# The hand-over from the dense layer to the experts: one weight load issued by ScalarE, one conversion and two squarings queued behind the last tile's routing

## The chip, the cores and the metric

The kernel runs on one core of a Trainium2 chip. The metric is device time in microseconds (us) of one execution, and the time of a version is the median of several executions. Besides, one execution was recorded by the hardware profiler; its trace gives the start and duration of the instructions on each engine: TensorE (PE, with its weight loads shown apart as PEld), VectorE (DVE), ScalarE (ACT), GpSimd (POOL) and SyncE (SP, which issues DMAs here). Three engines issue DMAs: SP (the queue called q1 in the trace), ACT (q10) and POOL (q0).

## The reference, cut to what matters

The computation is a chain of three layers on 1152 tokens: an attention with a top-32 mask, a dense gated layer, and a routed layer with 8 experts, of which each token goes to one. Only the routed layer and what stands just ahead of it bear on the change:

```
logits = x @ w_gate                       # x: 1152 x 512, 8 experts
expert_idx = argmax(logits, axis=1)
gate_w = probs[arange(N), expert_idx]     # probs = softmax(logits)
# each token gets the next free place of its expert: disp[e, counts[e]] = x[i]
h = maximum(einsum('ecd,edf->ecf', disp, w1), 0.0)     # w1: 8 x 512 x 1024
y = einsum('ecf,efd->ecd', h, w2)                      # w2: 8 x 1024 x 512
out[i] = gate_w[i] * y[expert_idx[i], pos[i]]
```

## The kernel before, in words

The tokens are worked in nine tiles of 128 rows (NT = 9). For each tile there is attention, then `norm`, then the dense layer `moe1`, then `dispatch`, which routes the tile's tokens. Instructions are given to a scheduler that fixes one order for each engine when the program is built; on the chip each engine then works strictly in that order and waits where data are missing. `tc.issue_after(ins)`, here wrapped as `after(t, name)`, puts what is traced inside it behind `ins` in the order of the engine of `ins`; it touches no other engine and waits for no result.

**Routing.** `dispatch(t)` transposes the layer's output (L490) and copies it (`xu`, L492, on ACT), multiplies it with the router (L504, PE), copies the logits (`lg`, L507, DVE), and finds the chosen expert: the maximum (L527), its place as a one-hot row (`key`, `k8`, `oh`, L534 to L541), the place in the expert's list by two small matmuls against the counts (`before`, `cum`, L544 and L545, PE), and the row number `slot` (L565). Beside it runs the softmax weight (`nm`, `ex` L532 on ACT, L550, L553, L556) and the row itself: its size by a square on ACT (L498), a power of two from it (L511 to L517), the upper half `yh` (L519, ACT) and the lower half `yl` (L520, DVE). When row and slot are there, GpSimd scatters the 128 rows to the table `disp` in DRAM (L567). The last tile (t = 8) does most of this on DVE, earlier tiles partly on GpSimd.

**First expert.** The rows of expert 0 that earlier tiles have put into its first 128 places (group "a") don't wait for the last tile: `gather("a", ...)` (L775, a transposing DMA, issued by ACT behind `xu`) and `notes("a", ...)` (L788, the rows' weights and token numbers, ACT as well) read them during the last tile's routing. Those that the last tile adds (group "b", at most 48 rows) are fetched after its scatter: POOL gathers them (`xb`, L830), SP transposes them (`xbT`, L834).

**Weights.** The 16 expert matrices (2 MB each, two per expert) are loaded in the order `ORDER`, called weights 0 to 15 here, each as two DMAs of 1 MB (`load`, L721, all issued by SP). `size(j, n)` squares a matrix on ACT (L734), sums over partitions on PE (L739) and makes a power of two on DVE (L737 to L749). `convert(j, n)` splits it into two float16 halves: the upper half partly on ACT (L759) and partly on DVE (L761), the lower half on DVE (L764). Weights 0 to 3 are converted in four pieces each (2 pieces at L759, 2 at L761, 4 at L764), later ones in two (1, 1 and 2). The raw buffer of weights n is free for weights n + 4 once it is converted; weights 4 take the buffer of weights 2, weights 5 that of weights 3. `fetch_w` issues the next load; SP's order after weights 4 is the gathers of experts 1 to 3 with `xbT` between them, and then weights 5 onward (`issue_after(last.ins)`).

**Products.** `up` and `down` are the two products of an expert (L847, PE), evacuated by ACT (`hE`, L857) and DVE (L858; `yT`, L866). PE's order at the hand-over is `up("a")`, `down("a")`, `up("b")`, `up(1)`, `down("b")`, `up(2)`, `down(1)` and so on, with `send` (transposes L885, ACT L887, a scatter to the output by POOL L889) between them.

Of the kernel before, what the change touches and what calls it, by code (L numbers as in the profile page):

```python
# [14 lines left out]
AF = mybir.ActivationFunctionType  # L15
OP = mybir.AluOpType
# [5 lines left out]
DM = H * D  # L22
# [3 lines left out]
NT = N // P  # L26
# [10 lines left out]
WA = 128  # L37
# [8 lines left out]
def tile_topk_attention__then__moe__then__moe_routed(  # L46
# [3 lines left out]
    nc = tc.nc  # L50
    w_gate, w_val, w_out = (a.bitcast(I32) for a in (w_gate, w_val, w_out))
    cap = int(capacity)
# [5 lines left out]
    disp = dram.tile([E * cap + 16, ROW], F32, name="disp")  # L58
# [364 lines left out]
    yx, late, behind = {}, [], {}  # L423

    def after(t, engine):

        return tc.issue_after(behind[t, engine].ins)
# [58 lines left out]
    def dispatch(t):  # L486
        y = yx.pop(t)
# [6 lines left out]
        yh, yl = (yd[:, i * DM // 2:(i + 1) * DM // 2].bitcast(F16) for i in range(2))  # L494
        nc.gpsimd.tensor_copy(yd[:, DM + 1:ROW], tok[:, t:t + 1])
        yn = route.tile([P, 8], F32, name="yn")
# [19 lines left out]
            invert(yn[:, 2:3], yn[:, 1:2])  # L516
        nc.vector.tensor_scalar(yn[:, 5:6], yn[:, 1:2], YS, None, op0=OP.mult)  # L517
        if t == NT - 1:
            nc.scalar.activation(yh, y, AF.Copy, scale=yn[:, 5:6])  # L519
            nc.vector.scalar_tensor_tensor(yl, y, yn[:, 5:6], yh, op0=OP.mult, op1=OP.subtract)  # L520
        else:
            nc.scalar.activation(y, y, AF.Copy, scale=yn[:, 5:6])
            nc.scalar.activation(yh, y, AF.Copy)
            nc.gpsimd.tensor_tensor(yl, y, yh, op=OP.subtract)
# [15 lines left out]
        ev = nc.vector if t == NT - 1 else nc.gpsimd  # L540
# [6 lines left out]
        pos = route.tile([P, 4], F32, name="pos")  # L547
# [10 lines left out]
        if t == NT - 1:  # L558
            nc.vector.tensor_scalar(had, lp[:, 2, 0:1], float(WA), None, op0=OP.min)
            nc.vector.tensor_scalar(rest, had, tok[:, 0:1], cap - 1.0, op0=OP.add, op1=OP.min)  # L560
            with after(t, "xu"):
                gather("a", 0, 0, WA, ew, nc.scalar)
                notes("a", 0, 0, WA, ew, nc.scalar)
        slot = route.tile([P, 1], I32, name="slot")
        ev.tensor_scalar(slot, pos[:, 0:1], pos[:, 1:2], pos[:, 2:3], op0=OP.add, op1=OP.add)  # L565
        nc.gpsimd.tensor_tensor(cum, cum, oh, op=OP.add)
        scat.append(nc.gpsimd.indirect_dma_start(  # L567
            out=disp, out_offset=bass.IndirectOffsetOnAxis(ap=slot[:, :1], axis=0),
# [73 lines left out]
    for p in range(NP):  # L642
        t, hp = divmod(p, 4)
# [12 lines left out]
    for t in range(NT):  # L656
        ew = nc.vector if t in (0, 8) else nc.gpsimd
        t0 = (4 * t + 5) * SL
        at(t0 + 1, ahead(norm(t, ew), 300), 1)
        at(t0 + (12 if t < NT - 1 else 18), ahead(moe1(t, ew), 0), 2.7)  # L660
        at(t0 + 10 + 4 * SL, ahead(dispatch(t), 0), 3 if t < NT - 1 else 1)
    live = []
    slot = 0
# [23 lines left out]
    ew = ctx.enter_context(tc.tile_pool(name="ew", bufs=1, reuse_waits="tile"))  # L687
# [7 lines left out]
    ORDER = [0, 1, 2, 3, 4]  # L695
# [13 lines left out]
    def raw_of(n):  # L709

        if n < 2:
            return slots[2 + n]
        return raws[n % 2 if n < 4 else n % 4]

    def load(j, n):
        e, w = divmod(j, 2)
        src = (w1, w2)[w][e].rearrange("(c p) f -> p c f", p=P)
        dst = raw_of(n).rearrange("p (c f) -> p c f", c=src.shape[1])
        m = src.shape[1] // 2
        for g in range(2):  # L720
            nc.sync.dma_start(dst[:, g * m:(g + 1) * m], src[:, g * m:(g + 1) * m])  # L721

    sized = {}
    BIG = 4 * DM
# [27 lines left out]
    def convert(j, n):  # L752

        raw, (hi, lo), sc = raw_of(n), place(j), sized.pop(j)
        k = 4 if n < 4 else 2
        for g in range(k):
            r = slice(g * 2 * BIG // k, (g + 1) * 2 * BIG // k)
            if 2 * g < k:
                nc.scalar.activation(hi[:, r], raw[:, r], AF.Copy, scale=sc[:, 7:8])  # L759
            else:  # L760
                nc.vector.tensor_scalar(hi[:, r], raw[:, r], sc[:, 7:8], None, op0=OP.mult)  # L761
        for g in range(k):
            r = slice(g * 2 * BIG // k, (g + 1) * 2 * BIG // k)
            nc.vector.scalar_tensor_tensor(lo[:, r], raw[:, r], sc[:, 7:8], hi[:, r], op0=OP.mult, op1=OP.subtract)  # L764

    meta, every, xgT, hE, yT2 = {}, {}, {}, {}, {}
# [3 lines left out]
    def gather(k, e, lo, hi, pool, eng):  # L770

        r = e * cap + lo
        n = -(-(hi - lo) // 16) * 16
        xgT[k] = pool.tile([P, 2 * KC, n], F16, name="xgT", bufs=1 if pool is ew else 3)
        g = eng.dma_start_transpose(out=xgT[k], in_=disp.bitcast(F16)[r:r + n, :2 * DM])  # L775
        return g

    def notes(k, e, lo, hi, pool, eng):

        for i, (o, m) in enumerate(chunks(hi - lo)):  # L780
            x = pool.tile([P, E, 2], F32, name=f"notes{i}", bufs=1 if pool is ew else 2)
            if k == 1 and not lo:
                eng.dma_start(x[:m, 1:], disp[:E * cap].rearrange("(e c) d -> c e d", c=cap)[lo + o:lo + o + m, 1:, DM:])
                every[i] = x
                for f in range(1, E):
                    meta[f, i] = x[:, f]
            else:
                eng.dma_start(x[:m, e], disp[e * cap + lo + o:e * cap + lo + o + m, DM:])  # L788
                meta[k, i] = x[:, e]

    def chunks(n):
        return [(o, min(P, n - o)) for o in range(0, n, P)]

    loaded = [0]

    def fetch_w():
        n = loaded[0]
        loaded[0] += 1
        if n < 2 * E:
            load(ORDER[n], n)  # L800

    for n in range(4):
        fetch_w()
# [10 lines left out]
    convert(1, 1)  # L814
    with after(NT - 1, "dve"):
        convert(2, 2)
    fetch_w()
    size(3, 3)
    pacc = ctx.enter_context(tc.tile_pool(name="pacc", bufs=3, space=PSUM, reuse_waits="tile"))
    pback = ctx.enter_context(tc.tile_pool(name="pback", bufs=2, space=PSUM, reuse_waits="tile"))  # L820
# [29 lines left out]
    def up(k, e, n):  # L850
        hE[k] = [eb.tile([P, NF2, n], F16, name=f"hE{i}", bufs=2 if n <= W else 1) for i in range(2)]
        for lo, hi in groups(NF2, n):
            a = pacc.tile([P, hi - lo, n], F32, name="acc")
            for c in range(lo, hi):
                product(a[:, c - lo, :], place(2 * e), (xgT[k][:, :KC], xgT[k][:, KC:]), KC, F2, c)
            hh, hl = (x[:, lo:hi, :] for x in hE[k])
            nc.scalar.activation(hh, a, AF.Relu)  # L857
            nc.vector.scalar_tensor_tensor(hl, a, 0.0, hh, op0=OP.max, op1=OP.subtract)  # L858
# [35 lines left out]

    with after(NT - 1, "pe"):
        up("a", 0, WA)
    with after(NT - 1, "dve"):
        convert(3, 3)
    last = gather(1, 1, 0, W, eb, nc.sync)
    rest_gather()  # L900
    notes(1, 1, 0, W, eb, nc.sync)
    for e in range(2, 4):
        last = gather(e, e, 0, W, eb, nc.sync)
# [5 lines left out]
    def ready():  # L909

        n = done[0]
        done[0] += 1
        if n >= 2 * E:
            return
        if n == 4:
            with after(NT - 1, "act"):
                size(ORDER[4], 4)
        if n + 1 < 2 * E:
            size(ORDER[n + 1], n + 1)
        convert(ORDER[n], n)  # L920
        fetch_w()
# [93 lines left out]
```

## Time and profile before

| | |
|---|---|
| median of 3 runs | 698.01 us (697.99 to 699.74) |
| the profiled execution | 697.47 us, of which its span is 695.6 us |
| busy in the span | PE 552.8, PEld 401.2, DVE 612.3, ACT 497.0, POOL 438.2 us |
| DMA | 80.00 MB, mean 115 GB/s over the span |
| granted TensorE clock, mean | 0.932 |

The span is what the trace covers; the profiled execution has 1.87 us more than its span. Times below count from the span's start. Busy time is an average over the three layers, so the rows are read stage by stage: the hand-over lies between about 540 and 575 us, the experts' products after it.

### The profile page before, as it was taken

The page shows a single profiled execution, that of the slowest core. Times are in us where ns is not written, and L with a number is a line of the kernel's source. Part 1 is how long each engine was busy: PE and PEld are TensorE (multiplying, and loading weights), DVE is VectorE, ACT ScalarE, POOL GpSimd, SP SyncE. Part 2 cuts the span into 40 slices and gives each one's busy share as a digit, 9 for nine tenths or more (in the row PEclk, how much of TensorE's full clock was granted, in tenths as well). Part 3 has the DMA queues.
Part 4 walks back from the last instruction along what each step waited for, and adds up shares of the span by engine and source line. Part 5 has one row for each costly group of instructions (what it writes and reads, how often), then busy time and mean ns, then how long its engine had stood idle before and what let it go on. Part 6 is the DMA issues. An engine that isn't in the chain of part 4 may idle for free.

```text
span 695.6 us, 12985 instructions
## 1 busy us (share of the span) xinstructions
PE 552.8 (79%) x4708; PEld 401.2 (58%) x4708; DVE 612.3 (88%) x1215; ACT 497.0 (71%) x959; POOL 438.2 (63%) x521
## 2 busy tenths in 40 slices
PE   1217425467687999999999999999999679999994
PEld 1106314344444666666666666665545469999994
DVE  3999999999999999999999999997158865999960
ACT  3456539569875888878789787887598438988821
POOL 3785889988895987877878779597531110023312
PEclk9999665588989999999999999999999889999998
DMA  8998171475000001000000000000850459999201
GB/s 236 264 327 279 34 243 44 128 228 192 17 1 23 9 31 43 16 32 10 31 8 16 32 9 24 1 2 16 302 197 1 151 125 389 309 328 347 96 21 39
DMA packets 47016, 80.00 MB, mean 115 GB/s; under 512 B 18732, under 2 KB 23340, under 8 KB 46946
## 3 DMA queue, kind: packets, MB, share of 16 engines
q1 hardware_dynamic: 43954, 74.02, 33.5%
q0 software_dynamic: 1792, 4.83, 1.9%
q8 instruction: 39, 0.64, 0.4%
q10 hardware_dynamic: 1200, 0.26, 0.2%
q14 instruction: 31, 0.25, 0.1%
HBM read 64.35 MB, written 12.27 MB: 110 GB/s over the span
## 4 chain that ended last, share of the span: by engine, by line
PE 31%; DVE 24%; issue 14%; POOL 13%; ACT 9%; DMA 7%; SPq 1%; POOLq 0%; ACTq 0%; DVEq 0%
PE pm L450 9%; PE pm L475 6%; DVE r L331 6%; DVE m L334 6%; PE acc L847 4%; POOL pp L351 3%; DVE wbig L155 3%; PE xps L382 3%; DMA wbig<-in_w_out_dram 3%; DVE wbig L157 3%; PE tp L374 2%; POOL out_dram L889 2%; PE tp L308 2%; DVE m L322 2%; DVE wbig L226 2%
## 5 line engine op out<-in xcount | busy, mean ns | idle before, releaser
L450 PE MATMUL pm<-wbig,xn 128*128 128x512 f16 x600 | 154.3, 390 | 6.9 <-ACT xn L420 3.5
L334 DVE MAX8 m<-r 128x8 f32<-128x576 f32 x216 | 156.5, 743 | 0.4
L847 PEld LDWEIGHTS <-split 128*128 128x128 f16 x1728 | 116.7, 100 | 13.7 <-issue 7.2
L308 PE MATMUL tp<-kst,qh 128*128 128x288 f32 (+1 forms) x160 | 64.2, 413 | 65.5 <-ACT s L310 21.4
L351 POOL TENSOR_TENSOR pp<-s,pp 128x576 f32<-128x576 f32 x72 | 102.9, 1442 | 10.1 <-ACT pp L350 9.6
L331 DVE MATCH_REPLACE8 r<-m,r 128x576 f32<-128x576 f32 x144 | 106.1, 738 | 0.0
L450 PEld LDWEIGHTS <-xn 128*128 128x128 f16 x648 | 63.4, 100 | 73.0 <-issue 14.2
L308 PEld LDWEIGHTS tp<-kst,qh 128*128 128x128 f32 (+1 forms) x160 | 32.6, 206 | 92.0 <-ACT s L310 29.0
L475 PE MATMUL pm<-wbig,hT 128*128 128x512 f16 x324 | 77.4, 380 | 7.3 <-DVE wbig L226 4.6
L310 ACT ACTIVATE s<-tp 128x288 f32<-128x288 f32 x144 | 54.7, 410 | 22.3 <-POOL pp L351 18.3
L889 POOL DMA_INDIRECT out_dram<-ob,tos x14 | 22.5, 1609 | 71.6 <-ACT ob L887 56.2
L764 DVE SCALAR_TENSOR_TENSOR split<-raw,sc,split 128x2048 f16<-128x2048 f32 (+1 forms) x32 | 65.8, 2077 | 0.3 <-ACT split L759 0.3
L374 PE MATMUL tp<-ident,pp 128*128 128x128 f32 x324 | 56.7, 294 | 11.0 <-ACT pp L356 10.5
L350 ACT ACTIVATE pp<-s,bias 128x576 f32<-128x576 f32 x72 | 51.9, 772 | 16.0 <-POOL bias L336 15.9
L847 PE MATMUL acc<-hE,split 128*128 128x168 f16 (+2 forms) x864 | 58.8, 228 | 4.0 <-ACT junk L734 1.3
L847 PE MATMUL acc<-xgT,split 128*128 128x168 f16 (+1 forms) x768 | 58.0, 239 | 4.3 <-DMA xgT<-disp 4.3
L734 ACT ACTIVATE junk<-raw 128x2048 bf16<-128x2048 f32 (+1 forms) x32 | 54.1, 1692 | 6.8 <-DMA raw<-in_w_dram 5.7
L356 ACT ACTIVATE pp<-pp,bias 128x576 f32<-128x576 f32 x72 | 56.3, 782 | 3.2 <-POOL pp L351 2.9
L375 ACT ACTIVATE pt<-tp 128x384 f32<-128x384 f32 x108 | 48.8, 492 | 11.7 <-PE tp L374 6.9
L374 PEld LDWEIGHTS tp<-ident,pp 128*128 128x128 f32 x324 | 41.3, 150 | 25.0 <-ACT pp L356 13.8
L382 PE MATMUL xps<-pt,vt 128*64 128x128 f32 (+1 forms) x800 | 55.7, 279 | 0.0
L322 DVE MAX8 m<-s 128x8 f32<-128x576 f32 x72 | 53.6, 745 | 1.8 <-ACT s L310 1.7
(203 smaller groups left out, 1230.4 us busy)
## 6 DMA issues: line engine op xcount, KB each, us to landing
raw<-in_w_dram SPq DMA_DIRECT2D x28, 1024.0 KB, 9.8
wbig<-in_w_out_dram SPq DMA_DIRECT2D x6, 1024.0 KB, 9.0
disp<-wraw SPq DMA_DIRECT2D x18, 257.0 KB, 5.4
qraw<-in_q_l_dram SPq DMA_DIRECT2D x72, 64.0 KB, 2.2
wraw<-in_w_gate_dram SPq DMA_DIRECT2D x8, 512.0 KB, 4.5
split<-in_w_dram SPq DMA_DIRECT2D x4, 1024.0 KB, 7.6
kraw<-in_k_l_dram SPq DMA_DIRECT2D x12, 288.0 KB, 4.1
wbig<-in_w_val_dram SPq DMA_DIRECT2D x3, 1024.0 KB, 8.0
```

The costliest lines, as they stand in the source:

```text
L308: nc.tensor.matmul(sp[:c1], x[:, i, :c1], kst[b, hp][:, i, c * HALF:(c + 1) * HALF], start=(n == 0), stop=(n == 1))
L322: nc.vector.max(m[:, i, 0], s[i])
L331: nc.vector.match_replace(r[i], m[:, i, n - 1], src, -3.0e38)
L334: nc.vector.max(m[:, i, n], r[i])
L351: nc.gpsimd.tensor_tensor(w, s[i], w, op=OP.subtract)
L356: nc.scalar.activation(pp[p][:, i], pp[p][:, i], AF.Exp, bias=bias[:, i, 0:1], scale=0.125, accum_out=sums[t][:, h:h + 1])
L374: nc.tensor.transpose(tp[:, i, :], p2[:, o:o + P], ident)
L382: nc.tensor.matmul(xps[t][rows, hp, c0:c1], v, w, start=(n == 0), stop=(n == 4))
L450: nc.tensor.matmul(a, xn[:, x + c, :], half(i, lo), start=(c == 0 and n == 0), stop=(c == KC - 1 and n == 2))
L475: nc.tensor.matmul(yps, hT[f // KC][:, KC * hi + f % KC, :], half(i, lo), start=(f == 0 and n == 0), stop=(f == NF1 - 1 and n == 2))
L764: nc.vector.scalar_tensor_tensor(lo[:, r], raw[:, r], sc[:, 7:8], hi[:, r], op0=OP.mult, op1=OP.subtract)
L847: nc.tensor.matmul(a, u[:, c, col * P:(col + 1) * P], v[:, c, :a.shape[-1]], start=(c == 0 and n == 0), stop=(c == nk - 1 and n == 2))
```

## The change

Four things are done. The load of weights 4 is issued by ACT instead of SP, and in ACT's order it is put behind the notes of group "a". The conversion of weights 3 was traced behind the last tile's last half `hT` (`behind[t, "dve"]`), and is now traced behind `slot`; as `slot` is an instruction of DVE, this moves DVE's pieces alone. The squares of weights 4 on ACT are put behind `yh` as well as behind `ex`. The rest of the diff hands out the instructions that these lines need.

```diff
@@ -516,7 +516,7 @@
         if t == NT - 1:
-            nc.scalar.activation(yh, y, AF.Copy, scale=yn[:, 5:6])
+            behind[t, "yh"] = nc.scalar.activation(yh, y, AF.Copy, scale=yn[:, 5:6])
             nc.vector.scalar_tensor_tensor(yl, y, yn[:, 5:6], yh, op0=OP.mult, op1=OP.subtract)
@@ -560,9 +560,9 @@
             with after(t, "xu"):
                 gather("a", 0, 0, WA, ew, nc.scalar)
-                notes("a", 0, 0, WA, ew, nc.scalar)
+                behind[t, "notes"] = notes("a", 0, 0, WA, ew, nc.scalar)
         slot = route.tile([P, 1], I32, name="slot")
-        ev.tensor_scalar(slot, pos[:, 0:1], pos[:, 1:2], pos[:, 2:3], op0=OP.add, op1=OP.add)
+        behind[t, "slot"] = ev.tensor_scalar(slot, pos[:, 0:1], pos[:, 1:2], pos[:, 2:3], op0=OP.add, op1=OP.add)
@@ -712,13 +712,13 @@
-    def load(j, n):
+    def load(j, n, eng=nc.sync):
...
         for g in range(2):
-            nc.sync.dma_start(dst[:, g * m:(g + 1) * m], src[:, g * m:(g + 1) * m])
+            eng.dma_start(dst[:, g * m:(g + 1) * m], src[:, g * m:(g + 1) * m])
@@ -781,23 +781,24 @@
-                every[i] = x
+                every[i], d = x, None
...
-                eng.dma_start(x[:m, e], disp[e * cap + lo + o:e * cap + lo + o + m, DM:])
+                d = eng.dma_start(x[:m, e], disp[e * cap + lo + o:e * cap + lo + o + m, DM:])
                 meta[k, i] = x[:, e]
+        return d
...
-    def fetch_w():
+    def fetch_w(eng=nc.sync):
         n = loaded[0]
         loaded[0] += 1
         if n < 2 * E:
-            load(ORDER[n], n)
+            load(ORDER[n], n, eng)
@@ -814,7 +815,8 @@
     with after(NT - 1, "dve"):
         convert(2, 2)
-    fetch_w()
+    with after(NT - 1, "notes"):
+        fetch_w(nc.scalar)
     size(3, 3)
@@ -894,7 +896,7 @@
     with after(NT - 1, "pe"):
         up("a", 0, WA)
-    with after(NT - 1, "dve"):
+    with after(NT - 1, "slot"):
         convert(3, 3)
@@ -913,7 +915,7 @@
         if n == 4:
-            with after(NT - 1, "act"):
+            with after(NT - 1, "act"), after(NT - 1, "yh"):
                 size(ORDER[4], 4)
```

## Rows read from the trace of the kernel before

**Rows 1.** The chain that ended last: start us, duration us, what

```profile
546.09 5.96 DMA xgT<-disp
...
560.12 1.06 POOL disp L567
...
563.27 4.42 DMA xb<-disp,rest
567.71 3.06 DMA xbT<-xb
```

**Rows 2.** Timeline of DVE: start us, us, line, operation, count

```profile
542.14 1.64 DVE L761 TENSOR_SCALAR split<-raw,sc 128x1024 f16<-128x1024 f32 x2
543.70 2.47 DVE L764 SCALAR_TENSOR_TENSOR split<-raw,sc,split 128x1024 f16<-128x1024 f32 x2
546.09 1.40 DVE L761 TENSOR_SCALAR split<-raw,sc 128x1024 f16<-128x1024 f32 x2
547.41 4.86 DVE L764 SCALAR_TENSOR_TENSOR split<-raw,sc,split 128x1024 f16<-128x1024 f32 x4
...
552.26 2.46 DVE L764 SCALAR_TENSOR_TENSOR split<-raw,sc,split 128x1024 f16<-128x1024 f32 x2
554.65 0.15 DVE L507 COPY lg<-px 128x8 f32<-128x8 f32 x1
554.73 0.13 DVE L874 CAST to<-notes 128x1 int32<-128x1 f32 x1
...
555.50 0.23 DVE L541 TENSOR_SCALAR oh<-rank,k 128x8 bf16<-128x8 f32 x1
...
558.42 0.26 DVE L565 TENSOR_SCALAR slot<-pos 128x1 int32<-128x1 f32 x1
558.60 0.74 DVE L520 SCALAR_TENSOR_TENSOR yd<-yx,yn,yd 128x512 f16<-128x512 f32 x1
```

**Rows 3.** Timeline of PE in the same stretch; in brackets idle before it

```profile
546.73 1.06 PE L504 MATMUL px<-rg,xu 128*128 128x8 f32 x8 [0.69 <-ACT xu L492]
...
557.80 0.17 PE L545 MATMUL px<-cum,ones 128*128 128x8 bf16 x1
...
561.96 4.79 PE L847 MATMUL acc<-hE,split 128*128 128x128 f16 x83 [0.55 <-DVE sc L742]
570.81 3.69 PE L847 MATMUL acc<-xbT,split 128*128 128x48 f16 x96 [4.05 <-DMA xbT<-xb]
```

**Rows 4.** Timeline of ACT in the same stretch

```profile
547.48 0.60 ACTq L788 DMA_DIRECT2D notes<-disp  x1
...
557.59 0.71 ACT L519 ACTIVATE yd<-yx,yn 128x512 f16<-128x512 f32 x1
```

**Rows 5.** Timeline of SP's DMA issues, asked in several stretches

```profile
546.23 0.37 SPq L721 DMA_DIRECT2D raw<-in_w_dram  x1
...
552.30 0.37 SPq L721 DMA_DIRECT2D raw<-in_w_dram  x1
...
570.51 12.36 SPq L721 DMA_DIRECT2D raw<-in_w_dram  x8
```

**Rows 6.** DMA issues by line from 500 us on: size, median us to landing

```profile
disp<-yd,slot POOLq DMA_INDIRECT x3, 2.9
...
notes<-disp ACTq DMA_DIRECT2D x1, 1.0 KB, 4.8
```

**Rows 7.** The same for the gather of expert 3 alone

```profile
xgT<-disp SPq DMA_TRANSPOSE x1, 3.8
```

**Rows 8.** Stretches: us, PE, PEld, DVE, ACT, POOL busy, PEclk, DMA share, GB/s

```profile
572.00:576.00 4.00, 4.00 (x92) 3.99 (x90) 0.56 (x1) 1.18 (x2) 0.00 (x0) 0.77 0.99 346
...
600.00:604.00 4.00, 4.00 (x60) 4.00 (x58) 3.90 (x11) 3.33 (x5) 0.00 (x0) 1.00 1.01 400
```

**Rows 9.** PE: the later product of group "b", and a later gap

```profile
582.65 1.72 PE L847 MATMUL acc<-hE,split 128*128 128x48 f16 x62
...
608.08 2.19 PE L847 MATMUL acc<-hE,split 128*128 128x168 f16 x28 [1.34 <-ACT junk L734]
```

## The prediction, made before the changed kernel was run

> **What bounds the kernel now.** I read the chain of waits first, then the timelines of DVE, PE, ACT and SP around the hand-over from the dense layer to the experts, then the landing times and the stretches after it. The chain shows one hand-over with little work in it: a gather of 5.96 us that PE waits for, then the last tile's scatter, its 4.42 us gather and its 3.06 us transposing DMA [rows 1]. PE's timeline gives the price: before the first product of group "b" it stands still for 4.05 us, until that DMA lands at 570.77 [rows 1, 3]. The stretches say how things stand later: from 572 us on PE, DVE and DMA are all close to full (at 600 to 604 us PE 4.00 and DVE 3.90 of 4 us, DMA share 1.01), so a start that comes earlier is worth something only if all three begin earlier [rows 8].
>
> Why is the scatter as late as 560.12? PE has the logits at 546.73 + 1.06 = 547.79 [rows 3]. DVE copies them at 554.65, because it first works off pieces of weights 2 and 3 without a pause: 4 at L761 and 8 at L764 [rows 2]. SP's second half of weights 4 goes out at 552.30, just as a piece ends on DVE; that load needs weights 2's buffer, so a piece of weights 2 came as late as 552.2, and pieces of weights 3 lie before it: the two are interleaved, and half of the twelve pieces are weights 3 [rows 2, 5].
>
> **The change part by part.**
>
> *Conversion of weights 3 behind `slot`.* Half of the 12 pieces leave the stretch. Start to start, L761 takes (547.41 - 546.09) / 2 = 0.66 us and L764 (552.26 - 547.41) / 4 = 1.21; 2 x 0.66 + 4 x 1.21 = 6.2 us [rows 2]. DVE then reaches `lg` at 554.65 - 6.2 = 548.5, after the logits' 547.8, so the whole 6.2 us come off. From `lg` to the end of `slot` it takes 558.68 - 554.65 = 4.03 us; 2.07 of these lie between the end of `oh` (555.73) and L545 on PE (557.80), which stood in PE's order among the matmuls of `up("a")` [rows 2, 3]. With these 2.07 us kept, slot ends at 552.5; without them at 550.4. I keep them, as the row has them.
>
> *`yh` before the squares of weights 4.* The scatter started 1.44 us after the end of `slot`, because `yh` ran on ACT only at 557.59 and `yl` on DVE from 558.60 [rows 2, 4]. Ahead of the squares, both are done by the time of `slot`. This takes off between 0.7 (the end of `yl`, 559.34, over that of `slot`, 558.68) and 1.44 us; I take 1.1, leaving 0.34 from slot to scatter. So the scatter goes at 552.9 instead of 560.12: 7.2 us earlier. It lands 2.9 us later [rows 6], at 555.8; weights 4 are then in flight, for which I allow 1 us. With 0.2 us of start, 4.42 and 3.06 us of the two DMAs [rows 1] the rows of group "b" are there at 564.5. SP's gathers and notes of expert 1 and 2, which it issues ahead of the transposing DMA, cost nothing: they fitted beside the 4.42 us, for that DMA followed at 567.71, right on 563.27 + 4.42 [rows 1].
>
> *The load of weights 4 on ACT.* Two DMA issues go from SP to ACT, at 0.37 us each on SP or 0.60 on ACT [rows 4, 5]. They cost nothing while ACT has nothing to do, and it hasn't between the notes (548.08) and the routing. But ACT stops at the issue until weights 2 are converted, at 548.5 in the new order. Behind it on ACT stand `ex` and `yh`; both need DVE results that come no sooner, so the stop costs 0, or at most the two issues, 1.2 us, if they come just then. The 1 us allowed above covers that. On SP the gathers were not held by the load: they waited for the scatter.
>
> What the move does is shift the time of the load. Before, its first half was issued 0.14 us after the gather of group "a", which took 5.96 us to land [rows 1, 5]; the gather of expert 3, with a load issued 1.58 us after its own issue, took 3.8 [rows 5, 7]. Now the load comes behind the notes and weights 2, 2.4 us or more after the gather. I take 3.8 us, so `up("a")` starts 2.1 us sooner; the other end is 0. The Trainium skill (DMA: Bandwidth & Descriptors, "Issuing engines are not separate DMA queues") says that DMAs of ScalarE and SyncE run on the same 16 engines and interleave, so that another issuer saves only the sequencer's time. By it alone the 2.1 us would be 0 and the time would be 692.9; no row here has a load from ACT.
>
> *What DVE does with weights 3 later.* Its 6.2 us now stand behind slot, 552.5 to 559.4 with `yl`. They cost nothing if the evacuation of `up("a")` is not held: PE's long run of `down("a")` began at 561.96 and ended at 566.75 [rows 3]; 2.1 us sooner it needs DVE at about 559.9, when weights 3 are through. If it is held, the 2.1 us go. Weights 3 themselves are used only in `down(1)`, four products after `up("b")`. Weights 5 want their buffer at about 563 (below).
>
> *The sum.* `down("a")` ends at 566.75 - 2.1 = 564.7 and group "b" is there at 564.5: `up("b")` starts 570.81 - 564.7 = 6.1 us sooner. The pause also had the clock granted at 0.77 on the mean from 572 to 576, between the levels of 1.2 and 2.4 GHz: 96 matmuls of group "b" took 3.69 us there, and 62 of the same width 1.72 at 582.65, so 2.66 for 96 [rows 3, 8, 9]. Without the pause that is 1.0 us more, in all 7.1 us. Behind it the loads of weights 5 onward, which start at 570.51 after the gathers behind the scatter [rows 5], start some 7 us sooner too, so DMA and DVE move along with PE. The profiled execution of 697.47 us would be 690.4; the median stands 0.5 above it, so I say 690.9 us.
>
> **Rivals.**
>
> *A: the first gather doesn't land sooner*, or DVE holds `down("a")`. Then only the pause of 4.05 us and its clock, 1.0, go: 692.9. For it speaks the skill's rule, against it the 3.8 us of rows 7.
>
> *B: routing stops at something else.* `to` (L874) stands right behind `lg` on DVE [rows 2] and needs the notes, which land 4.8 us after 547.48, at 552.3 [rows 4, 6]. With that order the rest of routing starts at 552.3, slot ends at 556.3, the scatter goes at 556.7, and group "b" is there at 568.3: 2.5 us gained on 570.81, with half of the clock's part 3.0, so 695.0. The same comes out if L545 still stands behind 62 matmuls of `up("a")`. Against it: with weights 3 gone the scheduler has no reason to place them so.
>
> *C: the train gives it back.* PE has gaps of up to 1.34 us among the later products, which end when ACT and DVE come through [rows 9]; three to five more of these, because conversions come in another order, eat 4 to 7 us: 695 to 698, no change. For it speaks that DVE and DMA are nearly full at 600 us [rows 8], against it that both are slack from 572 to 576 (DVE 0.56 of 4 us) and start earlier.
>
> *D: slower.* Weights 3 and then weights 4 stand on DVE ahead of the evacuation of `up("a")`. Each conversion is about 6 us; if both come first, DVE is through at 565 or later and the 4.79 us run of `down("a")` ends at 570 to 572. From 566.0 on as its start, group "b" starts later than today; at 568 the loss is 2 us, 700. Against it: weights 4 need their squares first, which now come later.
>
> **How the numbers follow.** My forecast (688.5 to 692.5) has 0.50, A 0.15, B 0.15, C 0.13 and D 0.07. The range goes from 687.5 (the 2.07 us at L545 and the 1 us of allowance can move `up("b")` no further than `down("a")`, but two later gaps can close) to 697.0, which leaves out D, half of C and a little below. A measurement tells 0.3%, 2.1 us, from no change, so faster means under 695.9: forecast, A, and most of B and a part of C, 0.80; same 0.13; slower 0.07.
>
> **What would show it.** `lg` at about 548.5 and `slot` at 550.4 to 552.5 on DVE; the scatter at about 553; the gather of "a" landing in about 4 us; no pause ahead of `up("b")`; weights 5 issued near 563. A late L545, DVE waiting in `to`, or a pause of PE behind `up("a")` would prove it wrong at that step; all of these right and an unchanged end would be C.

## The result, and the profile after

The changed kernel took 701.85 us (median of 17 runs, 698.87 to 705.14) beside 697.99 us for the kernel before on the same chip: ratio 1.006, 95% interval 1.0044 to 1.0077. It is slower by about 4 us, where 7 us less were forecast. The profiled execution took 701.71 us with a span of 699.8. (Ratios here and below are formed from all undisturbed runs and are not the quotients of the medians; in the table, conv_and_load_old_train is the only changed build with disturbed runs, 702.91 and 1153.3 us of its twelve, and its median is that of the other ten.)

In this trace the hand-over begins 1.01 us later than in the one before: the logits' matmuls start at 547.74 instead of 546.73 [rows 3]. That lies ahead of everything that was changed. Below, an *aligned* time has this difference taken off, and each experiment's is aligned in the same way (they begin between 2.1 us sooner and 2.3 us later).

The timeline of PE in the changed kernel (start us, us, line, operation, count; in brackets the idle time before it and what ended it), from the logits to product 2:

```profile
547.74 1.06 PE L504 MATMUL px<-rg,xu 128*128 128x8 f32 x8 [0.69 <-ACT xu L492]
550.38 2.40 PE L849 MATMUL acc<-xgT,split 128*128 128x128 f16 x21 [1.59 <-DMA xgT<-disp]
...
552.65 1.55 PE L849 MATMUL acc<-xgT,split 128*128 128x128 f16 x13
...
554.06 0.17 PE L545 MATMUL px<-cum,ones 128*128 128x8 bf16 x1
554.09 4.51 PE L849 MATMUL acc<-xgT,split 128*128 128x128 f16 x62
...
561.70 0.83 PE L849 MATMUL acc<-hE,split 128*128 128x128 f16 x12 [3.05 <-DVE hE L860]
...
562.42 6.42 PE L849 MATMUL acc<-hE,split 128*128 128x128 f16 x83
568.68 2.59 PE L849 MATMUL acc<-xbT,split 128*128 128x48 f16 x96
...
572.69 3.43 PE L849 MATMUL acc<-xgT,split 128*128 128x168 f16 x45
578.78 0.19 PE L739 MATMUL st<-s,ones 128*128 128x1 bf16 x2 [2.66 <-DVE s L737]
578.83 4.71 PE L849 MATMUL acc<-xgT,split 128*128 128x168 f16 x40
583.37 2.58 PE L849 MATMUL acc<-hE,split 128*128 128x48 f16 x96
...
587.60 1.97 PE L849 MATMUL acc<-xgT,split 128*128 128x168 f16 x25 [1.64 <-DVE hE L860]
...
629.23 1.61 PE L849 MATMUL acc<-hE,split 128*128 128x168 f16 x20 [0.70 <-DVE sc L743]
646.09 3.65 PE L849 MATMUL acc<-hE,split 128*128 128x168 f16 x48 [1.76 <-DVE sc L743]
660.18 4.00 PE L849 MATMUL acc<-hE,split 128*128 128x168 f16 x53 [2.55 <-DVE hE L860]
```

The 4.05 us pause ahead of `up("b")` [rows 3] is gone: group "b" follows the 83 matmuls of `down("a")` with no gap. In its place stand 3.05 us ahead of `down("a")`, and further on five waits that add up to 9.31 us. Behind the first two waits the granted clock is lower, as the view of stretches shows (PEclk is the third number from the end; the others are as in [rows 8]):

```profile
562.00:566.00 4.00, 4.00 (x49) 4.00 (x47) 1.83 (x10) 0.51 (x1) 0.00 (x0) 0.60 1.19 151
580.00:584.00 4.00, 4.00 (x52) 4.00 (x50) 3.83 (x8) 4.00 (x5) 0.41 (x1) 0.59 1.04 409
```

Timeline of DVE in the changed kernel at the hand-over:

```profile
549.54 0.15 DVE L507 COPY lg<-px 128x8 f32<-128x8 f32 x1
...
551.00 0.22 DVE L541 TENSOR_SCALAR oh<-rank,k 128x8 bf16<-128x8 f32 x1
...
554.68 0.27 DVE L565 TENSOR_SCALAR slot<-pos 128x1 int32<-128x1 f32 x1
554.86 1.41 DVE L761 TENSOR_SCALAR split<-raw,sc 128x1024 f16<-128x1024 f32 x2
556.18 4.87 DVE L764 SCALAR_TENSOR_TENSOR split<-raw,sc,split 128x1024 f16<-128x1024 f32 x4
560.96 0.68 DVE L860 SCALAR_TENSOR_TENSOR hE<-acc,hE 128x512 f16<-128x512 f32 x1
```

`oh` is ready at 551.22, but L545, which `slot` needs, stands behind 34 matmuls of `up("a")` on PE. Weights 3 then fill DVE from 554.86 to 560.96, and the evacuation of `up("a")`, whose matmuls end at about 558.6 (554.09 + 4.51), follows them.

ACT's DMA issues in the changed kernel, the gather of "a" and the load of weights 4; the gather lands where PE's wait ends, at 550.38:

```profile
547.09 1.36 ACTq L775 DMA_TRANSPOSE xgT<-disp  x1
...
549.12 0.96 ACTq L721 DMA_DIRECT2D raw<-in_w_dram  x2
```

POOL's timeline, the scatter and the gather of "b", which waits for the scatter's landing:

```profile
555.80 1.39 POOL L567 DMA_INDIRECT disp<-yd,slot  x1 [1.29 <-DVE split L761]
559.32 1.38 POOL L832 DMA_INDIRECT xb<-disp,rest  x1 [2.13 <-DMA disp<-yd,slot]
```

SP's issues, the transposing DMA of "b" and then the loads:

```profile
564.13 1.19 SPq L836 DMA_TRANSPOSE xbT<-xb  x1
...
567.31 9.97 SPq L721 DMA_DIRECT2D raw<-in_w_dram  x8
```

The last row's first load is that of weights 5: aligned 566.30, after 570.51 before [rows 5]. PE's last work ends at aligned 690.24, after 687.09 before: 3.15 us later, although `up("b")` starts at aligned 567.67, 3.14 us sooner. `up("b")` itself takes 2.59 us after 3.69 [rows 3], so it ends 3.14 + 1.10 = 4.24 us sooner, and the train behind it gave back 4.24 + 3.15 = 7.4 us.

### The profile page after: what moved, and what is told of

It reads as the page before. It is cut to its first block, busy times and chain, and to the rows that moved or that the text cites. A ratio compares the mean times of both kernels' runs of the same rounds, so it can differ in the third digit from the quotient of the medians.

```text
span 699.8 us, 12976 instructions
## 1 busy us (share of the span) xinstructions
PE 557.3 (80%) x4708; PEld 404.7 (58%) x4708; DVE 614.2 (88%) x1215; ACT 497.4 (71%) x959; POOL 433.2 (62%) x521
## 4 chain that ended last, share of the span: by engine, by line
DVE 35%; PE 25%; issue 21%; POOL 10%; ACT 5%; DMA 2%; SPq 1%; POOLq 0%; ACTq 0%; DVEq 0%
DVE r L331 10%; DVE m L334 9%; PE pm L450 8%; PE pm L475 6%; DVE wbig L155 4%; DVE m L322 3%; DVE wbig L157 3%; PE xps L382 2%; POOL out_dram L891 2%; POOL pp L351 2%; PE tp L308 2%; DVE wbig L226 2%; PE tp L374 2%; PE late L450 1%; POOL th L466 1%
## 5 line engine op out<-in xcount | busy, mean ns | idle before, releaser
L849 PEld LDWEIGHTS <-split 128*128 128x128 f16 x1728 | 119.3, 101 | 12.3 <-issue 10.1
L849 PE MATMUL acc<-hE,split 128*128 128x168 f16 (+2 forms) x864 | 60.5, 232 | 8.1 <-DVE hE L860 5.6
L891 POOL DMA_INDIRECT out_dram<-ob,tos x14 | 17.1, 1222 | 79.0 <-ACT ob L889 76.9
L849 PE MATMUL acc<-xgT,split 128*128 128x168 f16 (+1 forms) x768 | 60.5, 244 | 3.2 <-DVE hE L860 1.6
```

What stands on the lines that cost most here:

```text
L849: nc.tensor.matmul(a, u[:, c, col * P:(col + 1) * P], v[:, c, :a.shape[-1]], start=(c == 0 and n == 0), stop=(c == nk - 1 and n == 2))
```

## The experiments

The scheduler chooses the program's order of work on each engine anew for each build. The traces show that the order changed far behind the edits: before, PE's order had the sums of weights 5 (L739) among the products of `down("b")`; in the changed kernel they stand in the middle of `up(1)`, and ACT's and DVE's orders differ likewise up to the end. So most experiments hold the train's order fixed. "Old train" is the order of before from `down("a")` to the last `send`, on PE, DVE, ACT and SP; "new train" is that of the changed kernel. The edit is the same each time; `TRAIN` holds for each engine the places of the instructions in the order wanted, and its text moves the line numbers of the trace by about 8:

```diff
+    mark = len(tc.nc.cur_bb.bb.instructions)
     down("a", 0, WA)
...
+    traced = tc.nc.cur_bb.bb.instructions[mark:]
+    for engine, runs in TRAIN.items():
+        mine = [i for i in traced if str(i.engine) == "EngineType." + engine]
+        places = [n for r in runs.split() for n in range(int(r.split("-")[0]), int(r.split("-")[-1]) + 1)]
...
+        for a, b in zip(places, places[1:]):
+            tc.add_manual_dep(mine[b], mine[a].name, mybir.DependencyInfo(
+                mybir.DependencyClass.NoSync, mybir.DependencyReason.DATA), reason="order")
```

All of them in one table. Times are medians with that of the kernel before beside it; the three columns at the right are aligned and come from each profile: start of `up("b")`, first issue of weights 5, end of PE's last work. Each profile is one execution, and executions of one build differ by several us (698.87 to 705.14 for the changed kernel), so a difference of 1 or 2 us between two rows of these columns proves nothing by itself.

| run | us / before | ratio, 95% interval | `up("b")` | weights 5 | PE ends |
|---|---|---|---|---|---|
| kernel before (profile of before) | 698.01 | | 570.81 | 570.51 | 687.09 |
| changed kernel | 701.85 / 697.99 | 1.006 (1.0044 to 1.0077) | 567.67 | 566.30 | 690.24 |
| old_handover_new_train | 706.66 / 697.93 | 1.0098 (1.0069 to 1.0127) | 571.46 | 571.49 | 695.99 |
| new_handover_old_train | 696.20 / 697.93 | 0.9971 (0.9947 to 0.9995) | 567.62 | 566.17 | 685.03 |
| after_sums5_later | 702.01 / 697.74 | 1.0056 (1.003 to 1.0082) | 567.61 | 566.52 | 692.18 |
| conv_alone_old_train | 695.02 / 697.93 | 0.9931 (0.9904 to 0.9957) | 567.49 | 567.71 | 683.97 |
| load_alone_old_train | 701.95 / 697.74 | 1.0048 (1.0022 to 1.0073) | 574.05 | 574.17 | 690.06 |
| conv_and_load_old_train | 694.90 / 697.74 | 0.9952 (0.9922 to 0.9982) | 567.01 | 567.12 | 684.19 |
| evac_first_old_train | 701.00 / 697.93 | 1.0032 (1.0009 to 1.0054) | 566.51 | 566.06 | 689.40 |
| routing_first_old_train | 696.18 / 697.74 | 0.9962 (0.9934 to 0.999) | 568.18 | 568.25 | 685.89 |
| routing_first_gathers_behind | 698.37 / 698.85 | 0.9993 (0.9967 to 1.0019) | 566.41 | 568.50 | 687.88 |
| conv_alone_gathers_behind | 697.13 / 698.85 | 0.9984 (0.9959 to 1.0009) | 565.79 | 569.02 | 685.93 |
| routing_first_gathers23_behind | 696.12 / 698.85 | 0.9955 (0.9929 to 0.998) | 565.38 | 567.33 | 686.17 |
| conv_alone_weights5_early | 696.37 / 698.07 | 0.997 (0.9945 to 0.9995) | 566.15 | 564.80 | 686.04 |
| conv_alone_weights567_early | 695.50 / 698.44 | 0.9969 (0.9943 to 0.9994) | 566.04 | 564.67 | 684.21 |

### Is it the order of the train?

**new_handover_old_train**: the changed kernel, old train.

> The changed kernel, but from the second product of group a on, each of PE, DVE, ACT and SP works in the order that it had before the change. Theory 'order': the change gains at the hand-over and loses more in the order that the scheduler then chose for the experts' products, so this one is faster than before, near 694 us (3.1 us sooner at the first product of group b and 1.1 us of clock, as the changed kernel's trace has them). Rival 'supply': weights, DMA and DVE let the products run no sooner in whatever order; then it stays at 698 to 702. Rival 'held evacuation': the conversion of weights 3 ahead of the evacuation on DVE is the whole loss; then it is as slow as the changed kernel, 701 to 702.

**old_handover_new_train**: the kernel before, new train.

> The kernel before, but from the second product of group a on each engine works in the order of the changed kernel. Theory 'order': slower than before by the gaps that this order makes, some 5 to 7 us: 703 to 705. Rivals 'supply' and 'held evacuation': the order costs nothing by itself, 697 to 699.

Both ways agree on the direction. The new train alone makes the kernel before 6.8 us slower by the ratio (4.8 to 8.9), and taking it out of the changed kernel turns +0.6% into -0.3%. (That is 696.20 us and not the 694 of the theory: under the old train, too, a part of the gain was lost.) No run held a kernel in its own order, so what the holding costs by itself was not measured; as the two runs went opposite ways, it doesn't explain both. In the timeline of PE of the old hand-over under the new train the same places wait:

```profile
583.44 0.19 PE L747 MATMUL st<-s,ones 128*128 128x1 bf16 x2 [2.23 <-DVE s L745]
...
592.25 1.97 PE L855 MATMUL acc<-xgT,split 128*128 128x168 f16 x25 [1.66 <-DVE hE L866]
```

The changed kernel and new_handover_old_train have the same hand-over, so their rows show how the first two waits come about. In both, ACT is through with the squares of weights 5 at about 578.5 us. In the old train PE still has work then, and does the sums at 579.46 without a wait:

```profile
571.86 6.91 PE L857 MATMUL acc<-xgT,split 128*128 128x168 f16 x93
578.60 1.02 PE L857 MATMUL acc<-hE,split 128*128 128x48 f16 x34
579.46 0.19 PE L747 MATMUL st<-s,ones 128*128 128x1 bf16 x2
```

In the new train the sums stand in the middle of `up(1)`, and PE waits 2.66 us for them. On DVE the old train does the last two evacuations of `up(1)` at 579.06 and 579.77, ahead of converting weights 5 (from 580.80). The changed kernel converts first, and PE waits another 1.64 us; DVE in the changed kernel:

```profile
582.34 4.62 DVE L764 SCALAR_TENSOR_TENSOR split<-raw,sc,split 128x2048 f16<-128x2048 f32 x2
586.88 0.68 DVE L860 SCALAR_TENSOR_TENSOR hE<-acc,hE 128x504 f16<-128x504 f32 x1
```

**after_sums5_later**: the changed kernel with its own train, but the sums of weights 5 behind `up(1)` on PE (in TRAIN's row of PE, places 194 and 195 behind 295).

> The changed kernel with its own order of the train, but with the two sums of weights 5 on TensorE behind the last product of up(1) instead of in its middle. If most of the loss of the new order comes from that one place (2.66 us of waiting at 576.12 and the clock granted at 0.59 from 580 to 584), 697 to 699 after 701.8 for the changed kernel. If the loss is spread over the later products, because VectorE and ScalarE work in another order too, the wait only moves to the next place and the time is 700.5 to 702.5.

The second reading held. PE (its timeline again) runs through `up(1)`, and waits later, for DVE and for longer:

```profile
580.05 0.19 PE L747 MATMUL st<-s,ones 128*128 128x1 bf16 x2 [0.16 <-DVE s L745]
581.62 2.58 PE L857 MATMUL acc<-hE,split 128*128 128x48 f16 x96 [1.38 <-DVE hE L868]
...
588.88 3.68 PE L857 MATMUL acc<-xgT,split 128*128 128x168 f16 x25 [4.66 <-DVE hE L868]
```

The 4.66 us end, as the 1.64 did, when DVE evacuates `up(1)` behind the conversion of weights 5. So the loss is not one badly placed wait on PE. How it is shared among the orders of PE, DVE and ACT was not separated: the old order on one beside the new one on the others was not tried.

### Which part of the change does what?

**conv_alone_old_train**: only weights 3 behind `slot`.

```diff
-    with after(NT - 1, "dve"):
+    with after(NT - 1, "slot"):
         convert(3, 3)
```

> Only the conversion of weights 3 is moved behind slot; the load of weights 4 stays on SP, the squares of weights 4 stay behind ex alone, and the later products have the order of before. Theory 'order': routing ends some 6 us sooner, the first gather does not land sooner (6 us), so the gain is about that of the pause ahead of group b, 4 us less what DVE holds up: 694 to 697. Rival 'supply': 698. It also tells how much of the gain needs the load on ACT.

It has the lowest ratio of all, inside its forecast: 2.9 us under the kernel before in the median, 4.8 by the ratio. With 7 runs, its interval overlaps those of the next ones. The gather of "a" lands late here (2.15 us of waiting, `up("a")` at 553.32), so PE does the routing matmuls ahead of it, `slot` ends at 552.92 (aligned 551.64), and `down("a")` runs unhindered; a pause of 1.66 us stays ahead of `up("b")`. PE's timeline in this run:

```profile
550.99 0.17 PE L553 MATMUL px<-cum,ones 128*128 128x8 bf16 x1
553.32 7.59 PE L856 MATMUL acc<-xgT,split 128*128 128x128 f16 x96 [2.15 <-DMA xgT<-disp]
...
562.32 4.79 PE L856 MATMUL acc<-hE,split 128*128 128x128 f16 x83 [0.51 <-DVE hE L867]
568.77 2.60 PE L856 MATMUL acc<-xbT,split 128*128 128x48 f16 x96 [1.66 <-DMA xbT<-xb]
```

**load_alone_old_train**: only the load on ACT.

```diff
-    fetch_w()
+    with after(NT - 1, "notes"):
+        fetch_w(nc.scalar)
```

> Of the three parts the load of weights 4 on ScalarE alone, with the experts' train in the order of before. If the load does only what step 3 of the prediction says, the gather of group a lands about 2 us sooner (some 3.5 us after its issue), up(a) and down(a) end about 2 us sooner, and the pause ahead of up(b) grows by the same, since the rows of group b come as late as before: 697 to 699, no change. If the stop of ScalarE at the load's issue holds ex and yh, the scatter goes later than 560.1 by up to 1.2 us and the time is 698.5 to 700.

Slower than either reading. `up("a")` does start 2.7 us sooner (aligned 549.38), but its evacuations then come ahead of routing in ACT's order, as its timeline shows:

```profile
551.81 0.60 ACT L867 ACTIVATE hE<-acc 128x512 f16<-128x512 f32 x1 [7.21 <-PE acc L857]
554.49 0.60 ACT L867 ACTIVATE hE<-acc 128x512 f16<-128x512 f32 x1 [2.08 <-PE acc L857]
554.98 0.29 ACT L540 ACTIVATE ex<-lg,nm 128x8 f32<-128x8 f32 x1
```

`ex` waits behind the second of them, `yh` behind the first square of weights 4, and the scatter goes at aligned 561.50, 1.4 us later than before. The rows of group "b" come 3.2 us later, and the time follows.

**conv_and_load_old_train**: both edits.

> Conversion of weights 3 behind slot and the load on ScalarE, without the change to the squares, train in the order of before. The conversion alone gave 695.0, all three parts 696.2. If the sooner start of up(a) is what does harm (the last routing matmuls then stand among its products, slot comes at about 554.9 instead of 552.9, and the evacuation of up(a) waits for the conversion until 561), this is 696 again, with a pause of 3 us or more ahead of the bulk of down(a). If the squares behind yh are what does harm, it is 693.5 to 695.

The trace has the pause of the first reading, 3.10 us ahead of the bulk of `down("a")`, but the time, 694.9 us, falls into the range of the second. The ratio 0.9952 lies between those of new_handover_old_train (0.9971) and of the conversion alone (0.9931), and its interval overlaps both. So neither the squares' edit nor the load on ACT, beside the conversion, changes the time by an amount that these runs can tell.

**evac_first_old_train**: all three parts, and weights 3 also behind the evacuation of `up("a")`: `with after(NT - 1, "slot"), after("a", "hl"):`.

> As new_handover_old_train, and the conversion of weights 3 stands behind both evacuations of the first product of group a on DVE instead of behind slot alone. Theory 'order': the 3.05 us that PE waited behind that product and some 1.6 us of lowered clock go as well, 689 to 691, unless group b's rows are then not there; 691 to 693 if these are what it waits for. Rival 'supply': as new_handover_old_train. Rival 'held evacuation': this alone repairs it, 694 to 697.

A miss: 701.0 us. The second half of the evacuation came only 0.9 us sooner (aligned), because its relu on ACT stood behind the second square of weights 4 (559.27 to 561.18), and weights 3 and 4 then filled DVE without a break from 562.43 to 575.09, so that PE waited 4.41 us for `yT` ahead of `send("a")`. This is close to rival D, brought on by hand.

**routing_first_old_train**: all three parts, and `up("a")` behind L545 on PE (`with after(NT - 1, "pos"):` around it).

> All three parts with the train of before, and up(a) on TensorE behind the last routing matmul (L545 of the profile before) instead of behind the logits. up(a) starts about 1 us later (551.3), slot comes about 3 us sooner (about 552), the conversion is through at about 558.5 when up(a) ends, so the pause ahead of down(a) shrinks from 3.4 us to about 1 and down(a) runs at the higher clock: up(b) at 566 to 567 instead of 568.8, 693 to 694.5. If the transposing DMA of group b lands at 568.7 whatever the scatter does, as with the conversion alone, up(b) starts no sooner and it is 695 to 696.

`slot` comes at aligned 552.2 and the pause ahead of `down("a")` falls to 0.84 us and two of under 0.6, as expected, with its 83 matmuls at 4.79 us again. But `up("b")` starts at aligned 568.18, the second reading. The scatter and the gather of "b", though issued sooner, are slower (the view of DMA issues; at the end us to landing), after 2.9 [rows 6] and 4.42 us [rows 1]:

```profile
disp<-yd,slot POOLq DMA_INDIRECT x1, 5.3
xb<-disp,rest POOLq DMA_INDIRECT x1, 6.8
```

### What does a sooner start of `up("b")` bring?

**routing_first_gathers_behind, conv_alone_gathers_behind, routing_first_gathers23_behind**: the experts' gathers behind the transposing DMA of group "b" on SP, all of them or only those of experts 2 and 3.

```diff
-    last = gather(1, 1, 0, W, eb, nc.sync)
     rest_gather()
-    notes(1, 1, 0, W, eb, nc.sync)
-    for e in range(2, 4):
-        last = gather(e, e, 0, W, eb, nc.sync)
+    with tc.issue_after(behind["xbT"].ins):
+        last = gather(1, 1, 0, W, eb, nc.sync)
+        notes(1, 1, 0, W, eb, nc.sync)
+        for e in range(2, 4):
+            last = gather(e, e, 0, W, eb, nc.sync)
```

> routing_first_old_train, and on SyncE the gathers and notes of experts 1 to 3 behind the transposing DMA of group b. In that run the gather of group b took 6.8 us to land beside the gathers of experts 1 and 2, after 4.4 in the kernel before. If they share the same engines, it lands in about 4.4 us again and up(b) starts 1.5 to 2.3 us sooner: 693 to 694.5 after 696.2. If the gather of group b is slow for another reason, or up(1) now waits for expert 1's gather, which goes out 3 to 4 us later, it is 696 or more.

> conv_alone_old_train, and the gathers and notes of experts 1 to 3 behind the transposing DMA of group b. down(a) ends 1.66 us before the rows of group b are there, so at most 1.7 us come off: 693.3 to 694 after 695.0 if the gather of group b lands in about 4.4 us instead of 6.4; 695 to 696 if up(1) waits for expert 1's gather or the gather of group b is as slow as before.

> As routing_first_gathers_behind, but the gather and the notes of expert 1 stay ahead of the transposing DMA and only the gathers of experts 2 and 3 go behind it. If it is the number of gathers in flight that slows the gather of group b, about half of the gain: 694.5 to 695.5 after 696.2. If one gather beside it is enough to slow it, 696.

The mechanism is right and the gain fails to come. With no gather beside it, the gather of "b" lands in 3.1 us instead of 6.8 (first) and 2.8 instead of 6.4 (second), and `up("b")` starts 1.7 to 2.8 us sooner, up to 5.4 us sooner than in the kernel before. But the times are 698.37, 697.13 and 696.12. (In the third one the gather of "b" took 5.1 us beside the one gather, between the two; as `up("b")` started soonest of all there, its time says nothing about the gathers.) In the second one PE's timeline now has waits in `down("b")` and slower matmuls after them. ACT's first square of weights 5 waits 4.85 us for the load, until 574.21, and a relu of `up(1)` stands behind it; PE's two waits follow from these, the first through the evacuation and the second through the sums of weights 5:

```profile
577.46 1.02 PE L856 MATMUL acc<-hE,split 128*128 128x48 f16 x34 [2.09 <-DVE hE L867]
580.15 0.19 PE L747 MATMUL st<-s,ones 128*128 128x1 bf16 x2 [1.68 <-DVE s L745]
...
582.72 8.77 PE L856 MATMUL acc<-xgT,split 128*128 128x168 f16 x96
```

Its loads of weights 5 go out behind the gathers at aligned 569.02, only 1.5 us sooner than before.

**conv_alone_weights5_early, conv_alone_weights567_early**: on top of conv_alone_old_train, expert 1's gather ahead of the transposing DMA and behind it weights 5, gather 2, gather 3, weights 6 and 7; in the second one weights 5, gather 2, weights 6 and 7, gather 3. The diff is that of the second one.

```diff
-    for e in range(2, 4):
-        last = gather(e, e, 0, W, eb, nc.sync)
+    with tc.issue_after(behind["xbT"].ins):
+        five = fetch_w()
+        with tc.issue_after(five.ins):
+            last = gather(2, 2, 0, W, eb, nc.sync)
     with tc.issue_after(last.ins):
-        for _ in range(3):
-            fetch_w()
+        for _ in range(2):
+            seven = fetch_w()
+        with tc.issue_after(seven.ins):
+            last = gather(3, 3, 0, W, eb, nc.sync)
```

> conv_alone_old_train, with the load of weights 5 on SyncE right behind the transposing DMA of group b and ahead of the gathers of experts 2 and 3, which go behind it (expert 1's gather and notes stay ahead). With all gathers behind the transposing DMA, up(b) began 5 us sooner than in the kernel before and the time fell by under 2 us: waits for weights 5 took the rest, whose loads were issued no sooner. If those loads were the limit, they now go out near 564 instead of 567.7 to 569 and land some 5 us sooner, down(b) no longer waits, and the whole train moves with up(b): 692.5 to 694, where the conversion alone gave 695.0 and the kernel before 697.9. If something else holds the train (DVE's own order, the later loads), it stays at 695 to 697.

> As conv_alone_weights5_early, but the loads of weights 6 and 7 also go ahead of the gather of expert 3, which goes behind them; the gather of expert 2 stays between weights 5 and 6. In that run down(b) no longer waited and product 2 began about 5 us sooner than in the kernel before, but the loads of weights 6 and 7 went out only at 574.6, since SyncE was held 8.4 us at the two gathers, and TensorE waited 2.6 us for the sums of weights 6. If the order of the loads is what the train hangs on, the loads of 6 and 7 go out near 568 to 570, that wait goes, and the time is 692.5 to 694.5. If it is the 16 engines' throughput over the whole train, the wait moves to weights 7 or 8 and it stays at 695 to 697.

With weights 5 early the time is 696.37 us, the second reading. No wait is left in `down("b")`, and product 2 starts at 578.83 (aligned 578.61, before 584.24). Then the wait moves one load further. SP's issues in this run, which stood at two gathers for 8.42 us before weights 6:

```profile
565.02 1.02 SPq L729 DMA_DIRECT2D raw<-in_w_dram  x2
566.09 8.42 SPq L784 DMA_TRANSPOSE xgT<-disp  x2
574.56 7.13 SPq L729 DMA_DIRECT2D raw<-in_w_dram  x6
```

and PE's wait for the sums of weights 6:

```profile
588.94 0.19 PE L748 MATMUL st<-s,ones 128*128 128x1 bf16 x2 [2.56 <-DVE s L746]
```

With weights 6 and 7 early too, the waits come at 597.75 (1.55 us), 604.95 (2.57) and 636.55 (1.16), and PE ends at aligned 684.21: of 4.8 us at `up("b")` 2.9 are left. The time, 695.50 us, is that of the second reading: the median fell by 2.9 us, no more than with the conversion alone. In the kernel before, the changed one and this run alike the DMA share is 0.94 to 1.12 in stretches of 14 and 20 us from 566 to 640 us; here is one stretch of this run (columns as in [rows 8]):

```profile
600.00:620.00 20.00, 17.43 (x233) 16.85 (x230) 19.54 (x27) 17.46 (x20) 4.07 (x2) 1.00 1.11 329
```

DVE is busy for 19.54 of the 20 us, PE for 17.43.

## Why the prediction was wrong

**`lg` 6.2 us sooner: right.** Aligned 548.53, forecast 548.5.

**The load on ACT lets the gather of "a" land sooner: right, and a little more.** 3.25 us after its issue (forecast 3.8), so `up("a")` starts 2.7 us sooner than before (forecast 2.1). The time of the load goes with it. With the load on SP right beside the gather (conv_alone, 547.51 and 547.37) the gather took 5.9 us; with the load issued 2 us behind it from ACT, 3.2; and the gather of [rows 7], with a load from SP 1.58 us behind it, 3.8. The Trainium skill (DMA: Bandwidth & Descriptors, "Issuing engines are not separate DMA queues") says that DMAs run on the same 16 engines and interleave, whichever engine started them; nothing here speaks against it, but no run here shows it either, as the issuer and the time of the load changed together. That a sooner `up("a")` is worth something is another matter: conv_alone has none of it and the lowest ratio.

**`slot` and the scatter: the place right, the sizes short.** L545 did stand among the matmuls of `up("a")`, which by then ran at half the clock (granted 0.50 from 550 to 555 us): `slot` ends at aligned 553.94, forecast 552.5. From `slot` to the scatter 0.85 us pass, forecast 0.34; before, too, 0.78 us had passed between the end of `yl` at 559.34 and the scatter at 560.12 [rows 1, 2], which left no room for 0.34. The scatter's landing, the gather and the transposing DMA took 3.52, 4.81 and 4.0 us, where 4.1, 4.42 and 3.06 were put in. Together the rows of group "b" come at aligned 567.1, 2.6 us later than forecast.

**"What DVE does with weights 3 later costs nothing": wrong.** DVE was to be through at 559.4 and to be needed at 559.9. It was through at aligned 559.95, and the evacuation had been due since PE's last matmul of `up("a")` at aligned 557.6, since that started sooner. PE waited 3.05 us, and the 83 matmuls behind it took 6.42 us instead of 4.79 [rows 3], at a granted clock of 0.60. That is 4.7 us, which the text had as its condition ("if it is held, the 2.1 us go") but priced without the clock. DVE was not all that held it: the second relu of `up("a")` stood on ACT behind the second square of weights 4, which waited for its load until 557.93, and ran at 559.85. In evac_first_old_train, where the conversion is out of the way, the 83 matmuls start only 1.0 us sooner (aligned 560.42 after 561.41). The hold put the end of `down("a")` at aligned 567.67, forecast 564.7. By itself it decided little: the rows of "b" would have allowed 567.1.

**The pause ahead of `up("b")` goes, and its clock cost with it: right.** 2.59 us for the 96 matmuls, forecast 2.66. Altogether, `up("b")` starts 3.1 us sooner instead of 6.1, and ends 4.2 us sooner instead of 7.1.

**"So DMA and DVE move along with PE": this step failed, and it carries the sign.** It failed in two ways.

First, the order of the train did not stay. In the text it was kept as it was; in fact the scheduler chose it anew. Of the 7.4 us given back behind `up("b")`, 5.2 go to the new order (PE ends at 690.24, and at 685.03 in new_handover_old_train with the same `up("b")`), 2.2 were lost in the old one too. On the rows: PE's waits behind `up("b")` are 9.5 us in all, against 4.6 in that run; the 40 matmuls at 578.83 took 4.71 us where 93 such took 6.91 there, so 1.7 us more for the clock; and that run has a product of 8.77 us instead of 7.12, at a granted clock of 0.79, which takes 1.65 off: 4.9 + 1.7 - 1.65 = 5.0. The two runs with the trains exchanged show the cause. Rival C named this mechanism, at "4 to 7 us" and a chance of 0.13. The 5.2 us lie inside that; but the gain was 3 us smaller than forecast and 2.2 us went elsewhere, which made it slower instead of the same. Which of the edits changed the order, and why the scheduler prefers it, was not looked into.

Second, even the old train would not have kept the gain. Weights 5 went out 4.2 us sooner, not 7, since SP issues them behind the transposing DMA of group "b", which itself came 4.6 us sooner (aligned 563.12 after 567.71 [rows 1]). And the runs with `up("b")` 4.4 to 5.4 us sooner end between 0.8 us later and 2.9 us sooner on PE. Where weights 5 went sooner too, the next load, or DVE, is what PE waits for. [Rows 8] had shown DVE and DMA nearly full at 600 us. The text took slack of both from 572 to 576 as leave to move everything, and that is a misreading: DVE is busy for 0.56 of the 4 us there, but the DMA share is 0.99. That the DMA engines' throughput is the last limit is not shown: DVE is as full in places, and no run took work off either.

**What stays open.** A version that starts the loads of weights 5 to 7 sooner and also has DVE's order chosen for it was not tried. The lowest ratio measured, 0.9931, is that of the conversion alone under the old train; whether the scheduler would leave that order alone if only this edit were made was not tried either.

## What to carry to other kernels

When a scheduler orders a long stretch behind an edit, compare the engines' orders of the two builds before any sum is made, or hold the order fixed: an edge of order added at 550 us changed the work up to 680 us, and that cost 5.2 us where the edit under the old order gave 2.1 (PE's end at aligned 685.03 after 687.09). A sooner start is worth what the stream behind it (here loads, their issue order, the conversions) can follow. And a moved block of DVE work costs nothing only if it ends before its successor is due by the *new* times, with the lower clock that can follow a wait (0.60 after the 3.05 us here, 1.00 after the 1.64) in its price.

## What the runs showed of the hardware that was not expected

The same small DMAs are far apart in time. The scatter of group "b" took 2.9 us with the engines idle ahead of it [rows 6], 3.3 in the changed kernel, and 5.3 in routing_first_old_train, where weights 4 were still coming in at 345 GB/s or more until 556 us, 2.7 us after its start. Its gather took 2.8 to 3.1 us with no gather of an expert beside it and 4.9 to 5.1 beside one. Beside two it took 4.4 to 5.1 us in seven kernels, those before and after the change among them, and 6.4 to 6.8 in three others; what makes these differ is not shown. The price of one DMA taken from an idle stretch did not carry over to a new place.

SP stood longer at the issue of a transposing gather right behind loads: 8.42 us for two of them in conv_alone_weights5_early, against 3.1 for two in the runs that issue them with no load just ahead, and 1.4 to 2.2 for a single one at the hand-over. Every load queued behind them goes out that much later. What SP waits for there is not shown.
